# The integer addition that rounds the weights on VectorE, with a mask, four small copies and one weight piece moved, in an mLSTM cell followed by a squared-ReLU network

## The chip, the cores and the metric

The kernel runs on one core of a Trainium2 chip, in one launch. The core has five engines that each work through their own queue in order: PE (TensorE, matrix products), DVE (VectorE), ACT (ScalarE), POOL (GpSimd) and SP (SyncE, which here only issues DMAs). An instruction waits in its queue until the semaphores it names have come, and everything behind it in the same queue waits too. The metric is the device time of the launch in microseconds (us). All arithmetic of the result is in float32; the two weight matrices arrive as float64.

## The reference

What is computed, cut to what matters:

```python
# attention: 4 batches x 8 heads, 768 time steps, head width 40
for t in range(S):
    m_new = np.maximum(f_gate[:, :, t] + m, i_gate[:, :, t])
    f_stab = np.exp(f_gate[:, :, t] + m - m_new)
    i_stab = np.exp(i_gate[:, :, t] - m_new)
    m = m_new
    C = f_stab[:, :, None, None] * C + i_stab[:, :, None, None] * np.einsum('bhd,bhe->bhde', vt, kt)
    n = f_stab[:, :, None] * n + i_stab[:, :, None] * kt
    h_tilde = np.einsum('bhde,bhe->bhd', C, qt)
    denom = np.maximum(np.abs(np.einsum('bhd,bhd->bh', n, qt)[:, :, None]), 1.0)
    y[:, :, t] = 1.0 / (1.0 + np.exp(-o_gate[:, :, t])) * h_tilde / denom
# network: x is y as (3072, 320); w_in (320, 2048), w_out (2048, 320)
h = np.maximum(x @ w_in, 0.0)
return (h * h @ w_out).astype(np.float32)
```

## The kernel before

The recurrence is cut into 24 chunks `s` of 128 time steps (six for each batch). For a chunk the kernel loads keys, queries and values; lays the gates' running sums A along the rows (`load_A`, tile `A_bc`, a DMA); sets the entries above the diagonal to a very small number (`mask`, L414, one or two affine selects on POOL); takes exponentials with the bias `b` (`weigh`, L450, eight ACT instructions at L467, from chunk 8 on at L461 with the turned copy `b_R` of `b_T`); multiplies the scores into them (`weighted`, L542, DVE at L552), which gives P; and multiplies P with the values on PE (`attend`, L554; from chunk 6 on `attend_begin`, L612, and `attend_end`, L671). The state C goes from chunk to chunk on DVE (L586) and POOL (L589, L594), and POOL makes the weighted values `vw` (L481, L487). `normalise` (L733) divides on DVE (L737 to L747) and leaves `x_sb`, which PE turns for the network (`turn_rows`, L772, matmuls at L777).

In `attend_begin` the last DVE instruction, L628, reads one element of a PSUM bank that PE has just written, and the second half of the chunk's matmuls (L666 in `attend_end`) waits for it.

The network runs on groups of two chunks. Groups 0 and 1 go through `ffn1` (PE at L799 and L810, ACT at L823 and L829); later groups through a scheme with fewer products (`ffn1_begin`, `ffn1_open`, `ffn1_rows`, `ffn1_close`; PE at L966 and L1015, ACT at L979 and L1032, DVE at L998 to L1000 and L1033 to L1036).

The weights come as float64. The class `Rounding` turns them into float32 in 18 pieces: pieces 0 to 9 are `w_in` (128 rows x 512 words), pieces 10 to 17 are `w_out` (128 x 640). `fetch` (L201) loads a piece as pairs of 32-bit words, `words` (L211, L213) makes two float arrays `mag` and `low` on ACT, and `join` (L216) clamps `mag` (L222), shifts it (L226), puts the sign in (L227), all on DVE, and adds the words of `mag` and `low` as integers (L231, on POOL); then it fetches the piece four further on. `step` calls `words` so that they stay a piece ahead, then `join`. The array `mag` has two buffers of its own, and every third of the first twelve pieces uses borrowed room instead.

The order is written out by hand: what a Python statement emits first stands first in its engine's queue. A first part handles chunks 0 and 1. The loop over `u` from 0 to 7 (L1137) takes half a chunk at a time, `s = 2 + u // 2`: at even `u` it turns the rows of chunk s-1, takes the scores of chunk s, a quarter of `ffn1`, `weighted(s)` and `weigh(s + 1)`; at odd `u` it runs `attend(s)`, a `join`, `normalise(s)` and another quarter of `ffn1`. The list `NEXT` says how many pieces must be done by the end of each `u`. At u = 0 a `step` stands ahead of `weigh(3)`, and `mask(3)` is called inside `weigh(3)`. Each `fetch` stands in SP's queue behind the loads emitted before it.

After the loop four ACT copies (L1200) write `b_R`. The second loop (L1217) runs over parts `n` of the network, four to a chunk, `s = 6 + n // 4`. At the end of parts 0 to 4 it calls `step` until `LAST[n]` pieces are done, so piece 16 is joined at the end of part 0 and piece 17 at the end of part 2. Part 3 ends with `ffn1_close` of group 2, part 4 begins with `scores(7)` and `weighted(7)`, and part 5 holds `attend_begin(7)`. Parts 4 and 5 multiply with the first and the second half of `w_out` (L836).

Of the kernel before, what the change touches and what calls it, by code (L numbers as in the profile page):

```python
# [10 lines left out]
I32 = mybir.dt.int32  # L11
# [3 lines left out]
ALU = mybir.AluOpType  # L15
# [14 lines left out]
def kernel(  # L30
# [27 lines left out]
    nc = tc.nc  # L58
# [4 lines left out]
    PR = H // 2  # L63
# [110 lines left out]
    class Rounding:  # L174
# [41 lines left out]
        def join(self):  # L216
            n = len(self.b)
            dst = pieces[n][0]
            w = dst.shape[1]
            mag, low = (t[:, :w] for t in self.a[n])  # L220
            bits = mag.bitcast(I32)
            nc.vector.tensor_scalar(  # L222
                mag, mag, scalar1=word_as_float(0x38000000), scalar2=word_as_float(0x47EFFFFF),
                op0=ALU.max, op1=ALU.min,
            )
            nc.vector.tensor_scalar(bits, bits, scalar1=3, scalar2=None, op0=ALU.logical_shift_left)  # L226
            nc.vector.scalar_tensor_tensor(  # L227
                bits, in0=self.raws[n][:, :w, 1], scalar=-0x80000000, in1=bits,
                op0=ALU.bitwise_and, op1=ALU.bitwise_xor,
            )  # L230
            nc.gpsimd.tensor_tensor(dst.bitcast(I32), bits, low.bitcast(I32), op=ALU.add)  # L231
            self.b.append(None)
            if n != LENT - 1:
                self.fetch()
# [186 lines left out]
    def mask(s):  # L421

        A = st[s]["A"][0]
        if s < ROT:
            nc.gpsimd.affine_select(
                A[:], A[:], compare_op=ALU.is_ge, fill=-1e30, base=0, pattern=[[0, H], [1, P]], channel_multiplier=-1,
            )
            return
        for rows in HALVES:
            part = A[rows, :, DP : DP + P].rearrange("p x (late t) -> p x late t", late=2)  # L430
            nc.gpsimd.affine_select(  # L431
                part, part, compare_op=ALU.is_ge, fill=-1e30, base=0, pattern=[[0, PR], [0, 2], [1, DP]],
                channel_multiplier=-1,
            )
# [604 lines left out]
    def ffn1_square():  # L1039
        if "open" in st:  # L1040
# [4 lines left out]
            nc.scalar.activation(g4[:, :, :, P0], g4[:, :, :, P0], AF.Square)  # L1045
            nc.scalar.activation(g4[:, :, :, P1], g4[:, :, :, P1], AF.Square)

    def do(f, s):
        if 0 <= s < NT:
            f(s)  # L1050
# [86 lines left out]
    for u in range(8):  # L1137
        s = 2 + u // 2
        relu_half()
        if u % 2 == 0:  # L1140
            if u == 0:
                ffn1(0, 0)
            else:
                turn_rows(s - 1)
                scores(s)
                ffn1(u // 4, u % 4)
            if u == 2:
                rounding.words()
            weighted(s)
            if u == 0:  # L1150
                rounding.step()
            if u == 2:
                mask(s + 1)
                rounding.join()
                rounding.join()
                weigh(s + 1, masked=True)
                rounding.words()
            else:
                weigh(s + 1)
                square_half()  # L1160
        else:
            load_A(s + 2)
            for r in {1: (4,), 3: (5, 6), 5: (7,), 7: ()}[u]:
                load(r)
            if u == 5:
                for r in range(4, 8):
                    half_tanh(r)
            attend(s)
            if u == 3:
                square_half()  # L1170
            rounding.join()
            normalise(s)
            for r in {5: (8,), 7: (9,)}.get(u, ()):
                load(r)
            for r in {5: (7,), 7: (8,)}.get(u, ()):
                pair_up(r)
            if u > 4:
                load_o(2 * s)
                load_o(2 * s + 1)
            transposes(s + 1)  # L1180
            rounding.words()
            ffn1(u // 4, u % 4)
            square_half()
        if u < 4:
            load_o(4 + u)
        while rounding.done < NEXT[u]:
            rounding.step()
        if u in WIN_SUMS:
            sums_of_win(WIN_SUMS[u])
# [4 lines left out]

    for m in range(2):
        for own in range(2):
            x = PR * (m ^ own ^ 1)
            nc.scalar.copy(b_R[HALVES[m], :, :, own], b_T[HALVES[1 - own], :, :, x : x + PR])  # L1200
    spread_slots(1)
    banks.close()
    ps_h = ctx.enter_context(tc.tile_pool(name="ps_h", bufs=5, space=PSUM))
# [6 lines left out]
    for g in range(1, NG):  # L1210
        parts += [(2, g, i) for i in range(4)]
        if g + 2 < NG:
            parts += [(1, g + 2, i) for i in range(4)]
    LAST = (17, 17, 18, 18, 18)
    assert LAST[-1] == len(pieces)

    for n, (which, g, i) in enumerate(parts):  # L1217
        s, at = 6 + n // 4, n % 4
        if n == 5:
            brought.close()  # L1220
            late = ctx.enter_context(tc.tile_pool(name="late", bufs=1, side="right"))
        even = s >= 8 and s % 2 == 0
        fast = which == 1
        if at == 0:
            if s < 8 or even:
                do(scores, s)
            if even:
                do(turn_kq, s + 1)
            if s < 8 or even:
                do(weighted, s)  # L1230
        if at == 1:
            do(attend_begin, s)
            if even:
                do(lambda s: scores(s, ("h", "h")), s + 1)
            if fast:
                ffn1_rows(g, 0, True)
            do(attend_end, s)
            do(decays, s + 1)
            do(mask, s + 1)
            if n > 4 and not even and not fast:  # L1240
                do(turn_kq, s + 1)
            do(decay_C, s + 1)
            if s > X_SQ and not fast and not even:
                do(turn_squares, s - 1)
            do(store_num, s)
            do(load_num, s)
            do(load_squares, s + 2)
            if even:
                do(load_A, s + 2)
        if 5 <= n < 8:  # L1250
            sums_of_weights(n - 5)
        if n == 6:
            sums(1, slice(0, NPAIR), (1, 2))
        if n == 8:
            sums_of_weights(3)
            sums(1, slice(0, NPAIR), (3,))
        if n == 9:
            sums(1, slice(0, NPAIR), (4,))
        if which == 2 and i == 3 and g == NG - 2:
            sums(g + 1, slice(0, NPAIR), (2,))  # L1260
        if which == 2 and g > 1 and i < 2:
            sums(g, slice(0, NPAIR), (3 + i,))
        if n == 0:
            ffn1_begin(g)
            sums_of_x(g)
            sums_of_win(2)
        if at == 3 and s >= 8 and s % 2 == 0 and s // 2 - 1 < NG:
            sums_of_x(s // 2 - 1)
        if at == 2 and not fast:
            if even:  # L1270
                do(turn_squares, s - 1)
            if n > 4:
                do(scale_q, s + 1)
        if at == 3:
            if s % 4 == 3:
                for r in range(s + 1, min(s + 5, NT)):
                    half_tanh(r)
        if fast:
            if i % 2:
                ffn1_close(g, i // 2, i == 1)  # L1280
                if at == 1 and g > 2:
                    do(turn_kq, s + 1)
                    do(turn_squares, s - 1)
            else:
                ffn1_open(g, i // 2)
                if i == 0 and g > 2:
                    sums(g - 1, slice(0, NPAIR), (2,))
            if at == 2 and g > 2:
                do(scale_q, s + 1)
        elif g == 0:  # L1290
            ffn2(g, *divmod(i, 2))
        else:
            ffn2_fast(g, i)
        if at == 2:
            do(lambda s: weigh(s, masked=True), s + 1)
            ffn1_square()
            if n < 4:
                do(turn_kq, s + 1)
                do(scale_q, s + 1)
            if even:  # L1300
                do(weighted, s + 1)
            do(normalise_turned, s)
            do(store_rows, s)
            if not even:
                do(load_A, s + 2)
            if s > 6:
                do(load_o, s + 5)
            do(load_rows, s)
            if s == 6:
                do(pair_up, s + 3)  # L1310
        if s > 6 and at == (3 if even else 2):
            do(pair_up, s + 3)
        if s > 6 and at == 3:
            if s == 7:
                load(s + 3)
            do(load, s + 4)
        if n in (9, 25):
            spread_slots(2 + n // 25)
        if at == 0:
            ffn1_square()  # L1320
        if n < 5:
            while rounding.done < LAST[n]:
                rounding.step()
# [30 lines left out]
```

## Time and profile before

| what | value |
|---|---|
| median of 3 runs | 500.82 us (500.54 to 502.58) |
| profiled execution, its own time | 498.15 us |
| span of the profiled execution | 496.4 us |
| granted TensorE clock | 1.00 |
| L231 on POOL, 128x512 | x10, about 1.28 us each |
| L231 on POOL, 128x640 | x8, 1.55 us each (median) |
| L227 on DVE, 128x512 and 128x640 | 0.69 and 0.83 us |
| L1200 on ACT | x4, 0.27 us each |
| A_bc load, 512 KB | 5.5 to 6.5 us to landing |

The span is the time between the first and the last instruction on the core; 1.75 us of the execution lie around it. A line of the timeline gives start, duration, engine, source line, operation, output and inputs, shape and count; a bracket at its end says how long the engine was idle before it and what released it. A line of the waits gives the waiting engine and line, the awaited engine and line, the total in us, how often, and the longest.

### The profile page before, as it was taken

What the parts mean: (1) busy time and instruction counts of PE and PEld (TensorE: products, weight loads), DVE (VectorE), ACT (ScalarE), POOL (GpSimd) and SP (SyncE); (2) the same over time, 40 slices, a digit from 0 to 9 for tenths busy, and PEclk for the clock granted to TensorE, in tenths of its full rate; (3) what the DMA queues carried; (4) which work ended last, traced back from release to release, by engine and by line L of the source; (5) the groups of instructions that cost most, each with busy time, mean ns of one, the idle gap of its engine ahead of it and who ended that gap; (6) DMA issues with size and microseconds to landing.
All of it is one profiled execution on the core that took longest, in us unless ns stands there. A gap on an engine that the chain in (4) does not pass through costs nothing.

```text
span 496.4 us, 15227 instructions
## 1 busy us (share of the span) xinstructions
PE 487.0 (98%) x6169; PEld 452.5 (91%) x6169; DVE 346.3 (70%) x700; ACT 241.3 (49%) x530; POOL 224.5 (45%) x317
## 2 busy tenths in 40 slices
PE   9999999999999999999999999999999999999997
PEld 4877878897799999999999999999999999999997
DVE  8598969868977677767866866866866956735441
ACT  3657888754612551581561670561861560423300
POOL 3265744531489458458549438448544030020000
PEclk9999999999999999999999999999999999999999
DMA  9999797756597597688678578677766532200000
GB/s 188 207 229 219 238 217 159 208 90 129 117 188 156 128 174 181 124 152 176 138 144 180 130 145 176 153 138 161 155 125 142 116 74 80 55 15 15 3 26 28
DMA packets 196167, 68.02 MB, mean 137 GB/s; under 512 B 158704, under 2 KB 186064, under 8 KB 196096
## 3 DMA queue, kind: packets, MB, share of 16 engines
q1 hardware_dynamic: 190560, 57.50, 55.9%
q0 software_dynamic: 5440, 9.34, 8.0%
q8 instruction: 49, 0.80, 0.7%
q10 hardware_dynamic: 96, 0.20, 0.2%
q14 instruction: 22, 0.18, 0.1%
HBM read 54.71 MB, written 18.01 MB: 146 GB/s over the span
## 4 chain that ended last, share of the span: by engine, by line
PE 90%; DVE 4%; ACT 2%; issue 1%; DMA 1%; POOL 1%; SPq 0%; DVEq 0%; POOLq 0%; ACTq 0%
PE h_ps L890 35%; PE h_ps L966 24%; PE h_ps L1015 7%; PE h_ps L799 4%; PE h_ps L836 3%; PE numT L655 2%; PE numT L636 2%; PE hp L575 2%; PE idle L1059 1%; PE h_ps L810 1%; PE numT L666 1%; PE tp L530 1%; PE h_ps L530 1%; PE tp L504 1%; PE tp L538 1%
## 5 line engine op out<-in xcount | busy, mean ns | idle before, releaser
L890 PE MATMUL h_ps<-T,S 128*128 128x160 f32 x352 | 51.7, 300 | 0.0
L996 ACT COPY r_sb<-h_ps 128x512 f32<-128x512 f32 x18 | 10.5, 585 | 83.7 <-PE h_ps L966 83.7
L890 PEld LDWEIGHTS h_ps<-T,S 128*128 128x128 f32 x352 | 48.9, 190 | 0.4 <-ACT g_c L1032 0.2
L890 PE MATMUL h_ps<-w_out,g 128*128 128x160 f32 x336 | 49.2, 303 | 0.0
L890 PEld LDWEIGHTS h_ps<-w_out,g 128*128 128x128 f32 x336 | 46.1, 190 | 1.3 <-issue 0.7
L906 DVE TENSOR_TENSOR y_sb<-y_sb,h_ps 128x160 f32<-128x160 f32 x44 | 14.1, 320 | 47.5 <-PE h_ps L890 47.5
L431 POOL TENSOR_SCALAR_AFFINE_SELECT A_bc<-A_bc 64x512 f32<-64x512 f32 x32 | 25.2, 788 | 47.0 <-ACT kq L448 40.7
L966 PE MATMUL h_ps<-xT,w_in 128*128 128x128 f32 x320 | 43.0, 278 | 0.8 <-ACT r_sb L979 0.8
L966 PE MATMUL h_ps<-lent_t,w_in 128*128 128x128 f32 x320 | 42.2, 275 | 0.0
L966 PEld LDWEIGHTS h_ps<-xT,w_in 128*128 128x128 f32 x320 | 38.9, 192 | 2.4 <-issue 1.0
L1015 PE MATMUL h_ps<-xT,w_in 64*64 64x128 f32 x960 | 39.1, 272 | 0.0
L966 PEld LDWEIGHTS h_ps<-lent_t,w_in 128*128 128x128 f32 x320 | 38.9, 192 | 0.2 <-issue 0.2
L966 PE MATMUL h_ps<-lent_t 128*128 128x128 f32 x320 | 39.0, 275 | 0.0
L966 PEld LDWEIGHTS h_ps<-lent_t 128*128 128x128 f32 x320 | 37.3, 192 | 0.0
L461 ACT ACTIVATE A_bc<-A_bc,b_R 128x64 f32<-128x64 f32 (+1 forms) x128 | 35.7, 361 | 1.0 <-POOL A_bc L431 0.5
L1015 PEld LDWEIGHTS h_ps<-xT,w_in 64*64 64x64 f32 x960 | 34.8, 133 | 1.3
L340 POOL DMA_DIRECT2D va<-in_v_dram x56 | 34.3, 619 | 2.5 <-DMA va<-in_v_dram 1.4
L686 DVE STREAM_TRANSPOSE tn<-numT 128x256 f32<-128x256 f32 x36 | 14.0, 428 | 28.6 <-PE numT L636 19.8
L481 POOL TENSOR_TENSOR vw<-va,A_bc 128x328 f32<-128x328 f32 x13 | 10.7, 822 | 50.6 <-ACT A_bc L461 50.5
L799 PE MATMUL h_ps<-xT,w_in 128*128 128x256 f32 x128 | 29.9, 384 | 1.7 <-POOL w_in L231 1.1
L958 POOL TENSOR_TENSOR lent_t<-xT 128x128 f32<-128x128 f32 (+1 forms) x18 | 13.0, 738 | 38.5 <-DVE xT L769 38.5
L799 PEld LDWEIGHTS h_ps<-xT,w_in 128*128 128x128 f32 x128 | 23.5, 190 | 5.8 <-POOL w_in L231 1.5
(200 smaller groups left out, 1191.0 us busy)
## 6 DMA issues: line engine op xcount, KB each, us to landing
A_bc<-a_slots SPq DMA_DIRECT2D x32, 256.0 KB, 4.7
num_rows<-tn SPq DMA_DIRECT2D x18, 256.0 KB, 2.2
kq<-num_rows SPq DMA_DIRECT2D x72, 64.0 KB, 2.0
raw<-in_moe_w_out_dram SPq DMA_DIRECT2D x7, 640.0 KB, 4.2
kqT<-kq_rows SPq DMA_DIRECT2D x34, 128.0 KB, 3.0
og<-in_o_gate_dram SPq DMA_DIRECT2D x24, 160.0 KB, 5.3
out_dram<-y_sb SPq DMA_DIRECT2D x24, 160.0 KB, 3.1
raw<-in_moe_w_in_dram SPq DMA_DIRECT2D x7, 512.0 KB, 5.6
```

Source lines behind the costliest of these rows:

```text
L340: eng.dma_start(dst[HALVES[n], PR * (1 - late_keys) : PR * (2 - late_keys)], src[HALVES[late_keys], PR * m : PR * (m + 1)],)
L431: nc.gpsimd.affine_select(part, part, compare_op=ALU.is_ge, fill=-1e30, base=0, pattern=[[0, PR], [0, 2], [1, DP]], channel_multiplier=-1,)
L461: nc.scalar.activation(A[0][:, x, to], A[0][:, x, to], AF.Exp, bias=b_R[:, b, c, own, x : x + 1],)
L481: nc.gpsimd.tensor_tensor(d["vw"][:].rearrange("p (own x) d -> p own x d", own=2), d["va"][:].rearrange("p (own x) d -> p own x d", own=2) ...
L686: nc.vector.transpose(to[:, 2 * m : 2 * m + 2], d["numT"][m].rearrange("p c t -> p (c t)"))
L799: nc.tensor.matmul(hs[i][:, n, :], lhsT=w_in[:, a, fb * P : (fb + 1) * P], rhs=xT[:, :, a, :], start=(n == 0 and a == 0), stop=False,)
L836: nc.tensor.matmul(o_ps, lhsT=st["g2", g][:, fb, j * P : (j + 1) * P], rhs=w_out[:, fb, :], start=(fb == 0), stop=(fb == NF - 1),)
L890: nc.tensor.matmul(to, lhsT=lhsT[:, p], rhs=rhs[:, p, :], start=(start and p == 0), stop=(p == NPAIR - 1), skip_group_check=True,)
L906: add = lambda to, a, b: nc.vector.tensor_tensor(to, a, b, op=ALU.add)
L958: sub = lambda to, a, b: eng.tensor_tensor(to, a, b, op=ALU.subtract)
L966: nc.tensor.matmul(to[:, n, :], lhsT=lhsT[:, 4 * q + n, :], rhs=rhs, start=(start and n == 0), stop=True, skip_group_check=True,)
L1015: nc.tensor.matmul(to[cols, n, :], lhsT=w_in2[rows, 4 * q + n, cols], rhs=rhs, start=(start and n == 0), stop=True, skip_group_check=True,)
```

## The change

Four edits. The integer addition L231 goes from POOL's queue to DVE's, directly behind L227. At u = 0 `mask(3)` is emitted ahead of the `step` there, no longer inside `weigh(3)`. The four copies into `b_R` become `turn_halves` and are emitted in part 3. Piece 17 is joined at the end of part 4 (behind `weighted(7)`) and no longer at the end of part 2.

```diff
@@ join
-            nc.gpsimd.tensor_tensor(dst.bitcast(I32), bits, low.bitcast(I32), op=ALU.add)
+            nc.vector.tensor_tensor(dst.bitcast(I32), bits, low.bitcast(I32), op=ALU.add)
@@ ahead of do
+    def turn_halves():
+        for m in range(2):
+            for own in range(2):
+                x = PR * (m ^ own ^ 1)
+                nc.scalar.copy(b_R[HALVES[m], :, :, own], b_T[HALVES[1 - own], :, :, x : x + PR])
@@ loop over u
             if u == 0:
+                mask(s + 1)
                 rounding.step()
...
             else:
-                weigh(s + 1)
+                weigh(s + 1, masked=(u == 0))
                 square_half()
@@ between the loops
-    for m in range(2):
-        for own in range(2):
-            x = PR * (m ^ own ^ 1)
-            nc.scalar.copy(b_R[HALVES[m], :, :, own], b_T[HALVES[1 - own], :, :, x : x + PR])
     spread_slots(1)
...
-    LAST = (17, 17, 18, 18, 18)
+    LAST = (17, 17, 17, 17, 18)
@@ loop over n
+        if n == 3:
+            turn_halves()
         if n in (9, 25):
```

On DVE the addition is built as a custom operation over 16-bit elements: 128x1024 where POOL had 128x512 words, 128x1280 where it had 128x640.

## The prediction

> **What bounds the kernel now.** I read the page's busy times first, then PE's waits, then the timeline of 0 to 126 us engine by engine.
>
> ```profile
> PE 487.0 (98%) x6169; PEld 452.5 (91%) x6169; DVE 346.3 (70%) x700; ACT 241.3 (49%) x530; POOL 224.5 (45%) x317
> ```
>
> PE is busy for 487.0 of 496.4 us. About 3.3 us of the rest is the tail after its last matmul, so some 6 us of holes are all that a change off PE can win. PE's waits name the holes:
>
> ```profile
> PE tp L777 <- ACT g L823: 1.2, 1, 1.2
> PE h_ps L799 <- POOL w_in L231: 1.1, 1, 1.1
> PE idle L1059 <- DVE zeros L1054: 0.9, 1, 0.9
> PE h_ps L966 <- ACT r_sb L979: 0.8, 1, 0.8
> PE h_ps L799 <- ACT g L823: 0.6, 1, 0.6
> PE numT L636 <- DVE A_bc L552: 0.5, 1, 0.5
> PE tp L777 <- DVE x_sb L746: 0.4, 1, 0.4
> PE tp L777 <- DVE x_sb L747: 0.4, 1, 0.4
> PE numT L666 <- DVE kq L628: 0.3, 1, 0.3
> ```
>
> By the timeline they lie at 65.39, 50.75, 0.94, 99.71, 44.43, 122.30, 30.56, 31.35 and 123.84 us. From 124 to 400 us PE is never idle, so whatever is won or lost before 124 us stays to the end. The first row is mislabelled: L777 turns `x_sb`, whose L746 ends at 65.24, just ahead of 65.39.
>
> The stretch from 31.2 to 65.5 us holds the most (in order PE, PEld, DVE, ACT, POOL busy):
>
> ```profile
> 31.20:65.50 34.30, 31.30 (x213) 25.75 (x214) 31.27 (x50) 27.47 (x62) 21.60 (x20) 1.00 1.01 231
> ```
>
> DVE is busy for 31.27 of 34.30 us. But it is partly not working:
>
> ```profile
> 62.55 1.54 POOL L231 TENSOR_TENSOR w_out<-mag,low 128x640 int32<-128x640 int32 x1
> 62.66 1.46 DVE L740 SCALAR_TENSOR_TENSOR dm<-num,dm 128x8 f32<-128x8 f32 x1
> ...
> 39.97 1.35 POOL L425 TENSOR_SCALAR_AFFINE_SELECT A_bc<-A_bc 128x1024 f32<-128x1024 f32 x1
> 40.40 1.20 DVE L226 TENSOR_SCALAR lent_t<-lent_t 128x512 int32<-128x512 int32 x1
> ```
>
> L740 takes 0.17 us elsewhere and L226 0.43: each stands still until the POOL instruction ends.
>
> [...]L552 with a PSUM input (0.68 us always) never suffers. [...] No row shows the 16-bit addition.
>
> **The change part by part.**
>
> *The addition's price.* [...] On POOL 10 x 1.28 + 8 x 1.55 = 25 us vanish; on DVE 10 x 0.70 + 8 x 0.83 = 13.6 appear.
>
> *11.7 to 31.2 us.* Pieces 0 and 1 add 1.4 us; DVE idles for 5.6 us between them. Behind piece 1, `normalise(1)` moves 0.2 us, up against the mask of chunk 2, at 28.13 on POOL. If that now blocks L740 in place of L745, `x_sb` of chunk 1 is 0.3 us late for PE; otherwise 0. I take 0.1 lost.
>
> *31.2 to 65.5 us* decides. DVE runs from the first L222 at 31.21 to the end of L747 at 65.47: 34.26 us. Idle in it: 0.46 (for dC) and 1.58 (for ACT), 2.04. Excess over each form's shortest: L222 2.45 (0.59, 1.13, 0.17, 0.56), L226 4.81 (0.95, 0.77, 0.95, 0.76, 0.95, 0.43), L227 0.41, L739 0.17, L740 1.29, L747 0.42, together 9.55. Bare work is 34.26 - 2.04 - 9.55 = 22.67. Pieces 2 to 10 add 8 x 0.70 + 0.83 = 6.43. POOL keeps three `vw` (0.74), two masks (1.09), two pairs Cd and C (1.47), 7.34 us. Now the lock: if none of that blocks DVE, `x_sb` of chunk 3 is ready at 31.21 + 29.10 = 60.3, PE fills its three holes here (0.63 + 1.06 + 1.17) and gains 2.86. If all does, it is ready at 67.6 and PE loses 2.1. Walking the queues by hand with the trace's durations I get hits for nearly all. `vw` of chunk 2 slips in between L227 and the addition of piece 3 (0.65). Chunk 3's A_bc, issued at 31.17, lands 6.5 us later, at 37.7, so its mask meets piece 4 (0.95). Chunk 3's `vw`, Cd and C now meet piece 5 (3 x 0.55) rather than the idle 1.58 us. SP's next loads hang on the L227 of piece 4, which moves from 38.6 to 40.2, so chunk 4's A_bc lands near 47.6 and its mask meets piece 6 (0.95). The last three meet pieces 8 to 10 (1.8). Sum 6.0 (82%; before, 9.55 of 21.6, 44%). L747 then ends at 66.3, L746 at 66.1, and PE resumes 0.7 us later than at 65.39. On the way the hole at 44.43 closes (weigh of chunk 3 ends at 41.5, not 43.8), but `x_sb` of chunk 2 comes at 47.5 for a PE there at 46.8, and piece 6 at 51.0 for a PE that waited until 50.75. I take 0.7 lost, between 2.9 gained and 2.1 lost.
>
> *The mask.* On POOL nothing is left between chunk 2's `vw` and this mask, so once the addition is gone the edit moves no instruction past another: 0.
>
> *65.5 to 97 us.* DVE idles before L552 at 67.03 (1.56) and before L581 at 72.80 (2.69) and 88.20 (1.00). Pieces 11 to 15 (0.83 each, 4.2) fall into these and the L739 and L740 excess of 1.1 to 2.0 us a chunk. Taken at 0; without cover, at most 0.4 at the `x_sb` of chunk 4, which ends at 80.73 for a PE at 80.75.
>
> *The copies.*
>
> ```profile
> 97.93 1.11 ACT L1200 COPY b_R<-b_T 64x96 f32<-64x96 f32 x4
> 99.07 1.07 ACT L979 COPY r_sb<-h_ps 128x512 f32<-128x512 f32 x2
> ```
>
> Without them L979 can start 1.1 us earlier; its input is ready at about 97.9. The hole at 99.71 goes: 0.82 gained. In part 3 they land behind L1032 (115.22), where ACT is idle for 5.86 us ahead of L1043; their reader starts at 129.95. Cost 0.
>
> *Pieces 16 and 17.*
>
> ```profile
> 105.24 0.83 DVE L227 SCALAR_TENSOR_TENSOR mag<-raw,mag 128x640 int32<-128x640 int32 x1
> 106.09 0.16 DVE L628 TENSOR_SCALAR kq<-numT 1x1 f32<-1x1 f32 x1
> ...
> 117.38 0.49 DVE L222 TENSOR_SCALAR mag<-mag 128x640 f32<-128x640 f32 x1
> ...
> 123.63 0.16 DVE L628 TENSOR_SCALAR kq<-numT 1x1 f32<-1x1 f32 x1 [0.78 <-PE numT L666]
> ```
>
> Piece 16's addition stands ahead of L628, which moves from 106.25 (its end) to 107.1; PE wants it at 106.83. Loss 0.3. Piece 17 leaves the stretch ahead of L1033: 119.17 - 117.38 = 1.79 earlier, so P of chunk 7 comes at 121.0 and the hole of 0.52 closes. But behind P the piece takes 1.79 + 0.83 = 2.6, to 123.6, and L628 behind it ends at 123.8, where PE waits again, now with its first half done at 123.04. The hole moves and is not filled: 0 (0.5 gained if the piece is quicker). Part 5 needs the piece at about 126.7, in time.
>
> Sum: 0.1 + 0.7 - 0.82 + 0.3 = 0.3 us slower, 498.15 to 498.4. The runs' median stands 2.7 above the profiled execution; carried to it, 500.82 + 0.3 = 501.1.
>
> **Rivals.** *The lock rarely bites* (faster). If POOL's remaining work blocks DVE at 44% as before, 3.2 us, `x_sb` of chunk 3 ends at 63.5: gain 1.9, in all 2.3; at 20% or less PE's holes all close: -2.86 - 0.82 + 0.3 = -3.4, 497.4. For it: POOL loses over half its work here. Against: DVE loses its idle time, in which those blocks were hidden. [...] *Late DVE starves the fetches*: each `fetch` waits for an L227; it is inside my walk.
>
> **How the numbers follow.** What this kernel's measurement can tell from no change is 0.5%, 2.5 us. Forecast 0.50 (its own range 499.5 to 502.2: DVE's path from 1.6 better to 1.1 worse); the lock seldom bites 0.28 (497.0 to 498.3); slower 0.22 (503.4 to 507.5). For 8 in 10 the range runs from 497.4 to 504.0.
>
> **What would show it.** Right: L231 on DVE at 0.69 and 0.83; the waits L799 on POOL and L966 on L979 gone; a wait of L777 on `x_sb` near 66; L666 on L628 twice. Wrong: the addition above 0.95, or L777 at 63 or earlier, or a new hole after 124 us.

## The result, and the profile after

The changed kernel took 499.52 us (median of 22 runs, 496.96 to 509.31) beside 499.75 us (497.25 to 504.0) for the kernel before, run next to it: a ratio of 0.9984 with a 95% interval of 0.9963 to 1.0006. (Every ratio and every count of runs here leaves out the runs that took over 1.5% longer than the fastest of the same kernel, three of these 22, and so no ratio is the quotient of two medians.) That is no change within the 0.5% that the prediction set as its bound. The profiled span went from 496.4 to 496.8 us.

The page's busy times of the changed kernel show the work that moved. POOL lost 28 us (224.5 to 196.2) and DVE gained 4.1 (346.3 to 350.4), though the eighteen additions alone take 14.9 us there: the rest was time in which DVE instructions had stood still. L226 takes 9.8 us in all for 13.6 before, L739 and L740 together 2.0 for 6.6.

```profile
PE 486.7 (98%) x6169; PEld 452.6 (91%) x6169; DVE 350.4 (71%) x718; ACT 241.7 (49%) x530; POOL 196.2 (39%) x299
```

PE's waits in the changed kernel (waiting line, awaited line, us in total, times, longest):

```profile
PE tp L504 <- DVE num L581: 1.7, 2, 1.5
PE numT L666 <- DVE kq L628: 1.5, 2, 1.3
...
PE tp L777 <- DVE x_sb L747: 0.8, 2, 0.5
PE tp L777 <- DVE x_sb L746: 0.6, 2, 0.3
...
PE h_ps L799 <- DVE w_in L231: 0.3, 1, 0.3
```

Gone are L799 on POOL and on L823, L966 on L979, P of chunk 7, and L777 on the rows of chunk 3. The largest wait in their place is one that the list of before doesn't have, L504 on L581; L628 now holds PE twice, and L777 waits 0.29 and 0.50 us for the rows of chunk 2. Four holes on PE's timeline (start, duration, what, and in the bracket the idle time ahead of it with its releaser):

```profile
50.55 3.29 PE L799 MATMUL h_ps<-xT,w_in 128*128 128x256 f32 x14 [0.30 <-DVE w_in L231]
60.08 1.09 PE L504 MATMUL tp<-ident,kq 128*128 128x128 f32 x8 [1.48 <-DVE num L581]
106.56 0.44 PE L666 MATMUL numT<-vw,kq 64*64 64x41 f32 x16 [0.15 <-DVE kq L628]
123.56 0.44 PE L666 MATMUL numT<-vw,kq 64*64 64x41 f32 x16 [1.33 <-DVE kq L628]
```

As a mark for PE's progress I take the start of its 48 matmuls at L836 behind chunk 7: 124.89 us in the kernel before, 124.61 here. So the whole early stretch, where all four edits act, won 0.28 us.

And DVE's timeline of the changed kernel, where the new hole comes from:

```profile
54.88 0.69 DVE L227 SCALAR_TENSOR_TENSOR lent_t<-raw,lent_t 128x512 int32<-128x512 int32 x1
55.71 1.02 DVE L231 CUSTOM_DVE_ANT_0 w_in<-lent_t 128x1024 uint16<-128x1024 uint16 x1
56.65 0.95 DVE L222 TENSOR_SCALAR mag<-mag 128x512 f32<-128x512 f32 x1
57.63 0.43 DVE L226 TENSOR_SCALAR mag<-mag 128x512 int32<-128x512 int32 x1
58.09 0.69 DVE L227 SCALAR_TENSOR_TENSOR mag<-raw,mag 128x512 int32<-128x512 int32 x1
58.92 0.69 DVE L231 CUSTOM_DVE_ANT_0 w_in<-mag,low 128x1024 uint16<-128x1024 uint16 x1
59.53 0.49 DVE L581 TENSOR_TENSOR num<-hi,eA_T 128x328 f32<-128x328 f32 x1
```

L581 reads `hi`, which PE finished at 55.96 (L561, 54.84 + 1.12). It stands behind pieces 8 and 9 in DVE's queue and starts at 59.53, and only then is the PSUM buffer of `hi` free for PE's next transposes (both take turns in the same three buffers). The addition takes 0.69 us in nine of the ten pieces of 512 words; beside POOL's `vw` (55.22 to 56.17) the one at 55.71 took 1.02.

### The profile page after: what moved, and what is told of

Same layout as the page of the kernel before. It is cut to its first block, busy times and chain, and to the rows that moved or that the text cites. A ratio compares the mean times of both kernels' runs of the same rounds, so it can differ in the third digit from the quotient of the medians.

```text
span 496.8 us, 15232 instructions
## 1 busy us (share of the span) xinstructions
PE 486.7 (98%) x6169; PEld 452.6 (91%) x6169; DVE 350.4 (71%) x718; ACT 241.7 (49%) x530; POOL 196.2 (39%) x299
## 4 chain that ended last, share of the span: by engine, by line
PE 85%; DVE 5%; DMA 4%; SPq 2%; ACT 2%; issue 1%; POOL 0%; DVEq 0%
PE h_ps L890 34%; PE h_ps L966 23%; PE h_ps L1015 6%; PE h_ps L799 4%; PE h_ps L836 3%; PE numT L655 2%; PE numT L636 2%; PE hp L575 1%; PE tp L538 1%; PE numT L666 1%; PE h_ps L810 1%; SPq L706 1%; DMA kqT<-kq_rows 1%; PE tp L530 1%; PE h_ps L530 1%
## 5 line engine op out<-in xcount | busy, mean ns | idle before, releaser
L431 POOL TENSOR_SCALAR_AFFINE_SELECT A_bc<-A_bc 64x512 f32<-64x512 f32 x32 | 23.8, 743 | 57.6 <-ACT kq L448 56.6
L966 PE MATMUL h_ps<-xT,w_in 128*128 128x128 f32 x320 | 42.8, 278 | 0.0
L966 PE MATMUL h_ps<-lent_t,w_in 128*128 128x128 f32 x320 | 42.2, 275 | 0.0
L966 PEld LDWEIGHTS h_ps<-xT,w_in 128*128 128x128 f32 x320 | 38.9, 192 | 1.4 <-issue 1.0
L966 PEld LDWEIGHTS h_ps<-lent_t,w_in 128*128 128x128 f32 x320 | 38.9, 192 | 0.2 <-issue 0.2
L966 PE MATMUL h_ps<-lent_t 128*128 128x128 f32 x320 | 39.0, 275 | 0.0
L966 PEld LDWEIGHTS h_ps<-lent_t 128*128 128x128 f32 x320 | 37.3, 192 | 0.0
L799 PE MATMUL h_ps<-xT,w_in 128*128 128x256 f32 x128 | 29.6, 383 | 0.3 <-DVE w_in L231 0.3
L890 PE MATMUL h_ps<-w_out,g_c 128*128 128x160 f32 x192 | 28.0, 302 | 0.0
```

The source lines that it names most:

```text
L431: nc.gpsimd.affine_select(part, part, compare_op=ALU.is_ge, fill=-1e30, base=0, pattern=[[0, PR], [0, 2], [1, DP]], channel_multiplier=-1,)
L799: nc.tensor.matmul(hs[i][:, n, :], lhsT=w_in[:, a, fb * P : (fb + 1) * P], rhs=xT[:, :, a, :], start=(n == 0 and a == 0), stop=False,)
L890: nc.tensor.matmul(to, lhsT=lhsT[:, p], rhs=rhs[:, p, :], start=(start and p == 0), stop=(p == NPAIR - 1), skip_group_check=True,)
L966: nc.tensor.matmul(to[:, n, :], lhsT=lhsT[:, 4 * q + n, :], rhs=rhs, start=(start and n == 0), stop=True, skip_group_check=True,)
```

## Experiments

Two theories before the first runs. Theory A is the prediction's: the addition costs DVE about what leaving POOL gives back, and the three moves gain on their own. Theory B: taking from POOL 25 us of work that holds DVE up is a gain by itself, and something else eats it. "The lock" is the word of the prediction and the expectations for what the traces show: a DVE instruction stands still beside a POOL instruction, as L227 at 43.13 in the changed kernel, which took 1.25 us beside POOL's L594 (42.89 to 43.83) and 0.69 at its shortest. C stands in each expectation for the rival of that run.

### The addition alone, and the moves alone

`e1_add_only` is the kernel before with the first diff line of the change and nothing else; `e2_moves_only` is the changed kernel with that line undone:

```diff
-            nc.vector.tensor_tensor(dst.bitcast(I32), bits, low.bitcast(I32), op=ALU.add)
+            nc.gpsimd.tensor_tensor(dst.bitcast(I32), bits, low.bitcast(I32), op=ALU.add)
```

> Kernel before with the addition on VectorE and nothing else changed (mask inside weigh, copies between the loops, piece 17 at the end of part 2). Theory A (VectorE's own path paces PE up to 66 us; the lock relief only just pays for the additions there): L777 of chunk 3 comes 0.4 us later than before, the hole of 0.8 at L966 behind L979 stays, L628 behind piece 16 costs 0.3, and piece 17 with its addition ahead of P of chunk 7 widens the hole there from 0.5 to 1.3; in all 1.5 us slower than before (ratio 1.003). Theory B [...]: 1 to 2 us faster than before (ratio 0.996 to 0.998).

> The changed kernel with the addition put back on GpSimd; mask, copies and piece 17 stay moved. Theory A: chunk 3's mask now runs ahead of piece 4's addition, so the 0.6 hole at 44 us closes, ScalarE comes earlier to piece 6 and the 1.1 hole at 50.75 shrinks to 0 to 0.5; L979 0.8 gained; piece 17 without an addition on VectorE ends at 122.8 and L628 is in time, 0.5 gained; in all 2 to 3 us faster than before (ratio 0.994 to 0.996), and so 1.5 to 2.5 us faster than the changed kernel. Theory B: within 0.8 us of before (ratio 0.998 to 1.001).

The addition alone: 503.02 us, ratio 1.0069 (1.0037 to 1.0100). The moves alone: 498.14 us, ratio 0.9963 (0.9940 to 0.9985). So B falls: the addition on DVE is a loss by itself, and larger than A had it. PE's timeline of the addition alone, and its stretches (busy times of PE, PEld, DVE, ACT, POOL, then the granted TensorE clock, DMA share and GB/s), say why it is larger:

```profile
59.34 1.94 PE L504 MATMUL tp<-ident,kq 128*128 128x128 f32 x8 [1.48 <-DVE num L581]
61.07 4.49 PE L799 MATMUL h_ps<-xT,w_in 128*128 128x256 f32 x16
```

```profile
55.00:61.00 6.00, 4.52 (x34) 4.41 (x34) 5.76 (x9) 3.46 (x6) 2.57 (x3) 0.87 0.64 204
61.00:67.00 6.00, 6.00 (x29) 4.53 (x27) 3.82 (x10) 3.30 (x6) 0.65 (x1) 0.85 0.94 214
```

The hole of 1.48 us is the changed kernel's. But behind it the clock fell, and the same eight transposes take 1.94 us where the changed kernel's took 1.09; the next sixteen matmuls take 4.49 where 3.62 is usual. That is 1.7 us on top of the hole. Single executions stand up to 1.4 us apart before any edit acts, so I count from the scores of chunk 2 to the mark: the addition alone needs 95.66 us (31.20 to 126.86) where the kernel before needs 93.28 (31.61 to 124.89), 2.38 more, and without the 1.7 it would be 0.7 (an estimate). The moves alone need 90.92 (30.24 to 121.16), 2.36 less.

### No addition, and the addition twice

`e3_no_add` is the changed kernel without the addition, so L227 writes the weights itself (and L226 shifts by 0); `e4_add_twice` issues it a second time:

```diff
@@ e3_no_add
-                bits, in0=self.raws[n][:, :w, 1], scalar=-0x80000000, in1=bits,
+                dst.bitcast(I32), in0=self.raws[n][:, :w, 1], scalar=-0x80000000, in1=bits,
...
-            nc.vector.tensor_tensor(dst.bitcast(I32), bits, low.bitcast(I32), op=ALU.add)
@@ e4_add_twice
-            nc.vector.tensor_tensor(dst.bitcast(I32), bits, low.bitcast(I32), op=ALU.add)
+            for _ in range(2): nc.vector.tensor_tensor(dst.bitcast(I32), bits, low.bitcast(I32), op=ALU.add)
```

> The changed kernel without the integer addition on any engine: the sign instruction L227 writes the weights straight into their place and the shift L226 shifts by 0, so the low words are left out and the weights have other values; every other instruction is as in the changed kernel. Theory A: VectorE's path is 6.4 us of additions shorter by 66 us, PE's holes at 44, 50, 60 and 65 us all close, and L628 waits only about 0.5 us behind piece 17 and not at all behind piece 16: 3.5 to 4.5 us faster than before (ratio 0.991 to 0.993). Theory C (the holes do not hang on VectorE's path, but on loads and on ScalarE): less than 1.5 us faster than before.

> The changed kernel with each integer addition done twice on VectorE, one right behind the other, the same result written again. Theory A: another 6.4 us on VectorE's path by 66 us, nearly all of it on PE's as well, 0 to 1 us between 66 and 97, and 0.8 more at each of the two L628: 7 to 9 us slower than the changed kernel (ratio to before 1.013 to 1.018). Theory C: hidden but for the two L628, 1.5 to 3 us slower than the changed kernel.

Without it: 495.4 us, ratio 0.9913 (0.9882 to 0.9944), mark 119.82. Twice: 512.53 us, ratio 1.0260 (1.0223 to 1.0297), mark 136.64. So the first set of additions costs 0.7% and the second 2.8%, four times as much. PE's timeline and stretches of the doubled one:

```profile
64.49 1.97 PE L504 MATMUL tp<-ident,kq 128*128 128x128 f32 x8 [3.31 <-DVE num L581]
...
117.02 0.61 PE L666 MATMUL numT<-vw,kq 64*64 64x41 f32 x16 [1.95 <-DVE kq L628]
135.59 0.44 PE L666 MATMUL numT<-vw,kq 64*64 64x41 f32 x16 [1.32 <-DVE kq L628]
```

```profile
61.00:67.00 6.00, 2.69 (x12) 2.48 (x12) 5.69 (x10) 1.09 (x3) 0.99 (x1) 0.63 0.79 249
67.00:75.00 8.00, 8.00 (x47) 6.14 (x47) 6.03 (x12) 4.89 (x11) 2.03 (x2) 0.85 1.44 175
```

Over half of the second set's price is the clock, 0.63 and 0.85 in these stretches. One minus a run's mean granted clock, times its span, estimates what it lost to the clock; I call it the shortfall. On average it is 0.7 us without the addition, 1.5 in the changed kernel and 8.8 with the addition doubled. So some 7.3 of the second set's 13.8 us (2.8%) are the clock's, and 0.8 of the first set's 3.6. What is left, 6.5 and 2.8, is still twice as much for the second set, which found less idle and standing time on DVE; neither is paid in full, since ten additions at 0.69 and eight at 0.83 are 13.5 us. A is right in direction and rank in both; its 7 to 9 us for the second set left the clock out, and without the clock 6.5 is near them. (Without the addition the weights have other values; whether that bears on the clock is not shown.)

### Each move by itself, on the kernel before

`e6_mask_only`, `e7_copies_only` and `e8_piece17_only` each take one of the other three edits of the change, with the addition on POOL:

```diff
@@ e6_mask_only
+                mask(s + 1)
                 rounding.step()
...
-                weigh(s + 1)
+                weigh(s + 1, masked=(u == 0))
@@ e7_copies_only: the loop of four copies behind the loop over u
-                nc.scalar.copy(b_R[HALVES[m], :, :, own], b_T[HALVES[1 - own], :, :, x : x + PR])
...
+        if n == 3:
+            turn_halves()
@@ e8_piece17_only
-    LAST = (17, 17, 18, 18, 18)
+    LAST = (17, 17, 17, 17, 18)
```

> The kernel before with chunk 3's mask ahead of the step at u = 0, and nothing else. Theory A (with the addition on POOL, the mask waited there behind piece 4, and the exponentials of chunk 3 behind it): the wait of L777 at 44.43 us (0.63) goes, and PE stands 0.3 to 0.8 us earlier at 66 us; ratio to before 0.998 to 1.000. Theory C (the place of the mask costs nothing, as the prediction put it for the changed kernel): PE stands within 0.2 us of before at 66 us.

> The kernel before with the four copies of b in part 3, and nothing else. Theory A (they delay L979 by 1.1 us, and their new place is idle): the wait of L966 on L979 (0.82 at 99.71 us) goes, no wait appears in part 3 or behind, and PE stands 0.8 us earlier at 120 us; ratio to before 0.998 to 0.999. Theory C (another input of L966 is late anyway): a wait of 0.3 us or more stays at L966.

> The kernel before with piece 17 joined at the end of part 4, and nothing else; its addition stays on POOL. Theory A (the DVE part of the piece, 1.8 us, fits between P of chunk 7 and L628): the wait of 0.52 us for P of chunk 7 goes and that at L628 (0.28 at 123.84) goes too, PE stands 0.5 to 0.8 us earlier at 125 us; ratio to before 0.998 to 0.999. Theory C (the hole moves to L628 as it did with the addition on DVE): a wait of 0.3 us or more at L628 and PE within 0.3 us of before.

*The mask*: 498.38 us, ratio 0.9962 (0.9941 to 0.9984), more than A gave it, and about all that the three moves gain together. The timelines of POOL and ACT with the mask alone:

```profile
36.32 1.28 POOL L425 TENSOR_SCALAR_AFFINE_SELECT A_bc<-A_bc 128x1024 f32<-128x1024 f32 x1
...
37.64 2.46 ACT L467 ACTIVATE g_c<-A_bc,b_T 128x128 f32<-128x128 f32 x8 [0.77 <-POOL A_bc L425]
```

Before, the mask ran at 39.97 and the exponentials at 41.35, behind piece 4's addition on POOL. With the exponentials 3.7 us earlier the hole of 0.63 at 44.43 is gone, and the one at L799 fell from 1.06 to 0.70. From the scores of chunk 2 to L777 of chunk 3 PE needs 32.54 us (30.83 to 63.37) for 33.78 (31.61 to 65.39).

*The copies*: ratio 0.9987 (0.9960 to 1.0014), too small for the runs. In the trace the wait at L966 is gone and none appears in part 3: PE goes from L777 of chunk 5 to L836 in 20.55 us (96.57 to 117.12) for 21.59 (95.26 to 116.85). The mark itself, 125.19, is not early as A had it: behind the hole of 1.16 at L777 of chunk 3 the clock was 0.80 from 67 to 75 us in this execution.

*Piece 17*: ratio 1.0004 (0.9976 to 1.0031). The wait for P of chunk 7 is gone; a wait of 0.58 at L628 stays, which A said would go. From L836 to the mark PE needs 7.23 us (118.11 to 125.34) for 8.04, so A's sum holds and not its claim that all holes close. The mark itself, 125.34, is late for the same reason as with the copies (the stretch stands at the end of this document).

By the runs the three moves sum to -0.38 - 0.13 + 0.04 = -0.47%, and together they measured -0.37%.

### Pieces 16 and 17 added on POOL

`e5_tail_on_pool` is the changed kernel with one line edited:

```diff
-            nc.vector.tensor_tensor(dst.bitcast(I32), bits, low.bitcast(I32), op=ALU.add)
+            (nc.gpsimd if n > 15 else nc.vector).tensor_tensor(dst.bitcast(I32), bits, low.bitcast(I32), op=ALU.add)
```

> The changed kernel with the additions of pieces 16 and 17 back on POOL, the other sixteen on DVE. Theory A (behind these two pieces the addition itself delays L628): both waits of PE at L666 on L628, 0.33 us at 106.56 and the one at 123.56, go, and PE stands 0.4 to 1.0 us earlier at 124 us than with the changed kernel: ratio to before 0.996 to 0.998. Theory C (the tail has cover, and the loss is all before 66 us): both waits shrink by under 0.2 us together and PE stands as with the changed kernel.

Ratio 0.9989 (0.9960 to 1.0018): the runs don't tell it from the changed kernel. In the trace the first wait at L628 is gone and the second fell from 1.33 to 0.36; from the second half of chunk 6 (first L666) to the mark PE needs 19.01 us (107.22 to 126.23) for 20.36 (104.25 to 124.61). So behind these two pieces the addition costs 1.35 us, more than A's 0.4 to 1.0. The mark itself is late, 126.23, because in this execution the clock fell behind the 1.58 us hole at L504 (0.57 from 61 to 67 us).

### The new hole

`e10_piece9_later` is the changed kernel with piece 9 behind L581 and L586, and so piece 10 behind `normalise` of chunk 3:

```diff
-    NEXT = (5, 8, 10, 11, 12, 13, 14, 16)
+    NEXT = (5, 8, 9, 11, 12, 13, 14, 16)
...
             if u == 2:
                 mask(s + 1)
                 rounding.join()
-                rounding.join()
```

> The changed kernel with piece 9 joined at u = 3 (behind attend of chunk 3), and so piece 10 behind normalise of chunk 3. Theory A (the 1.48 us hole at L504 comes from L581 queued behind two joins): that hole goes, L799 waits 0.4 to 1.3 us for piece 9 in its place, L777 of chunk 3 comes 0.2 to 1.1 us earlier than with the changed kernel; ratio to before 0.996 to 0.999. Theory C (L581 is late for another reason, its input or the lock): a hole of 1 us or more stays at L504.

PE's timeline:

```profile
60.29 3.29 PE L799 MATMUL h_ps<-xT,w_in 128*128 128x256 f32 x14 [0.72 <-DVE w_in L231]
64.58 0.55 PE L777 MATMUL tp<-ident,x_sb 128*128 128x128 f32 x3
...
98.30 5.47 PE L966 MATMUL h_ps<-xT,w_in 128*128 128x128 f32 x32 [2.14 <-ACT g L823]
```

The hole at L504 is gone, 0.72 at L799 came for it, and L777 is 1.24 us earlier (64.58 for 65.82): that L581 was late because of the pieces ahead of it is shown. Yet the ratio is 1.0012 (0.9979 to 1.0044; A had 0.996 to 0.999, and the interval still reaches into it). In the trace a new hole of 2.14 us opens at 98.30, with a clock of 0.72 from 98 to 104 us. ACT's timeline names it:

```profile
95.81 0.79 ACT L211 ACTIVATE mag<-raw 128x640 f32<-128x640 f32 x1 [2.13 <-DVE w_out L231]
...
97.18 1.07 ACT L823 ACTIVATE g<-h_ps 128x512 f32<-128x512 f32 x2
```

With the pieces one place later, ACT stands in L211 for a free `mag` buffer, which an addition on DVE must release, and L823 behind it frees PE's PSUM late.

### Two better orders

`e11_moves_swap` is the moves alone with the second of these edits; `e9_mixed` has both:

```diff
@@ e9_mixed
-            nc.gpsimd.tensor_tensor(dst.bitcast(I32), bits, low.bitcast(I32), op=ALU.add)
+            (nc.vector if n in (5, 6) else nc.gpsimd).tensor_tensor(dst.bitcast(I32), bits, low.bitcast(I32), op=ALU.add)
@@ both
-            rounding.join()
-            normalise(s)
+            if u == 3: normalise(s)
+            rounding.join(); (u == 3) or normalise(s)
```

> The three moves with every addition on POOL, and at u = 3 normalise ahead of the join. Theory A: the hole of 1.17 us at L777 of chunk 3 goes, those of 0.76 and 0.89 stay, PE stands 0.9 to 1.2 us earlier at 124 us than with the moves alone; ratio to before 0.993 to 0.995. Theory C (the lock moves the loss): a hole of 0.6 us or more between 55 and 70 us.

> The three moves, with the addition on POOL except for pieces 5 and 6, which are added on DVE, and at u = 3 normalise ahead of the join. Theory A (each of the three holes left with the moves alone is one late item: x_sb of chunk 2 behind piece 5's addition on POOL 0.76, piece 6 itself 0.89, x_sb of chunk 3 behind piece 10 1.17): they shrink to under 0.8 us together, no hole over 0.6 is left, PE stands 2 to 3 us earlier at 124 us than with the moves alone (121.2), ratio to before 0.990 to 0.993. Theory C (the lock moves the loss elsewhere): holes of 1.5 us or more in sum stay and the ratio is not under 0.995.

`e11_moves_swap`: 495.21 us, ratio 0.9899 (0.9841 to 0.9957), mark 120.45. `e9_mixed`: 496.77 us, ratio 0.9916 (0.9874 to 0.9957), mark 119.72. Both beat the kernel before and lie under the changed kernel's interval; their own intervals overlap. PE's timeline of the second:

```profile
48.35 3.29 PE L799 MATMUL h_ps<-xT,w_in 128*128 128x256 f32 x14 [0.17 <-DVE w_in L231]
61.96 0.55 PE L777 MATMUL tp<-ident,x_sb 128*128 128x128 f32 x3
```

L777 of chunk 3 waits no more in either; the holes of 0.76 at chunk 2's rows and 0.89 at L799 shrank to none and 0.17 in `e9_mixed`, and were none and 0.69 in `e11_moves_swap`, with piece 5 and 6 still on POOL. A's reading of the 1.17 is shown (the swap alone closes it); of the 0.76 it isn't, since that hole went without the edit made for it, and ahead of the swap. The moves alone, then the swap:

```profile
46.04 0.52 PE L777 MATMUL tp<-ident,x_sb 128*128 128x128 f32 x3 [0.76 <-DVE x_sb L746]
46.37 0.55 PE L777 MATMUL tp<-ident,x_sb 128*128 128x128 f32 x3
```

So the swap is judged from these rows on. From there to the mark PE needs 75.12 us with the moves alone (46.04 to 121.16), 74.08 with the swap (46.37 to 120.45) and 73.81 with both edits (45.91 to 119.72): the swap gives 1.04, and DVE for two pieces 0.27. A had the mark 0.9 to 1.2 us earlier with the swap and 2 to 3 with both; it came 0.71 and 1.44 earlier. By the runs, six and thirteen, the two kernels lie 0.6% and 0.5% under the moves alone; the traces account for a third and about half of that. A's forecast that no hole over 0.6 is left missed: L628 waits 0.61, and ahead of the edits L777 of chunk 1 waits 0.90 (1.05 with the swap alone).

### Filling the holes

That the clock falls behind a hole was seen, not tested. `e12_holes_filled` tests it on the changed kernel:

```diff
-            transposes(s + 1)
-            rounding.words()
+            if u == 3: idle(3)
+            transposes(s + 1); rounding.words()
...
-            do(attend_end, s)
+            idle(2) if n == 5 else None; do(attend_end, s)
```

> The changed kernel with idle matmuls on PE (0.44 us each) in its two longest holes: three ahead of the transposes L504 of chunk 4 (hole of 1.48 us) and two ahead of the second half of chunk 7 (1.33). They are shorter than the holes, so PE goes on at the same events. Theory A (a hole above about a microsecond often brings the granted clock down for some microseconds after it): of the changed kernel's runs 3 in 19 had a mean granted clock of 0.999 or more; here at least half have, and the median falls 0.7 to 1.5 us under the changed kernel's, ratio to before 0.995 to 0.997. Theory C (the clock falls for another reason): the share stays under 30% and the ratio between 0.998 and 1.001.

The idle matmuls ran faster than in the expectation, and covered about 0.6 and 0.4 us; 0.88 and 0.94 of the two holes stayed. The mean granted clock was 0.999 or more in 11 of 22 runs, where it was in 3 of 19 of the changed kernel's, as A had it. The median didn't follow: 499.07 us, ratio 0.9984 (0.9956 to 1.0013), as for the changed kernel itself, and A's 0.7 to 1.5 us are not shown. The falls summed in the last section cost 1.7 or 3.4 us in a profile, so at 1.7 with the runs under 0.999 going from 16 of 19 to 11 of 22 about 0.6 us was to be expected (an estimate), which this interval can't tell from nothing. So the link from hole to clock is supported; what it costs the median of the changed kernel is open.

## Why the prediction was right

Forecast was no change, 501.1 us from 500.82; measured was no change, -0.16% (-0.37% to +0.06%). The 1.6 us between 501.1 and 499.52 are mostly the kernel before, which stood at 499.75 in this series. By the steps:

- **The addition's price** came as forecast: 0.69 and 0.83 us in the median (three of the eighteen, each beside a POOL instruction, took 1.02 to 1.57). The forecast was the author's estimate, for no row of before shows the operation. An addition above 0.95, which the prediction held possible, falls with it. Not priced was the start: L231 begins 0.83 us after L227 (58.09 to 58.92), where the next instruction behind an L227 began 0.61 after it, so a 512 piece costs DVE 0.83 and not 0.70, and a 640 piece 0.96 for 0.83 (0.96 and 0.75 from start to start, 61.95 to 62.91 to 63.66, for the 0.75 of one instruction alone): 9 x 0.13 = 1.2 us more up to 65.5.
- **31.2 to 65.5 us**: the sum came out near, from two errors that cancel. The additions took 7.6 and not 6.43; the blocks took 4.2 (excess over each form's shortest: L227 0.43 and 0.56, L222 0.50, 0.14 and 0.53, L226 0.41 and 0.56, L747 0.77, L231 0.33) and not 6.0, and 0.56 more was idle for ACT ahead of piece 2's addition. By these three terms the end of L747 would stay at the 66.3 that was forecast; it came at 65.91, and the other 0.4 us are not accounted for. `x_sb` of chunk 3 came at 65.67 (65.18 + 0.49) for 66.1, and L777 at 65.82: 0.43 lost for 0.7. The term is right, its place is not: the prediction followed DVE's queue to `normalise` and never asked who waits for L581 on the way. PE was late by 1.48 us at L504, and so found `x_sb` ready. It was this step, "resumes 0.7 us later than at 65.39" for want of `x_sb`, that named the wrong wait.
- **The holes on the way** went as walked: 44.43 closed, `x_sb` of chunk 2 at 47.15 (forecast 47.5; its last part, L747, only at 48.15), piece 6 at 50.50 with PE at 50.55 (51.0), chunk 3's mask at 37.54 (37.7).
- **11.7 to 31.2 us**: 0.1 lost was forecast; L777 of chunk 1 came at 30.59 for 30.56. Nothing was lost that a single execution can show.
- **The mask at 0** holds for the changed kernel: with the addition alone it ran at 36.79 without being moved. It was worth 0.38% only while the addition stood on POOL. Two edits of this change buy the same microsecond; that is read from these traces, for the changed kernel without this edit was not run.
- **The copies** gained as forecast: L966 runs in one piece from 97.27, and the copies lie at 115.62 beside idle ACT.
- **Pieces 16 and 17**: L628 ended at 106.51 (107.1 was forecast), with PE 0.27 early where it had been 0.60 early at L966: 0.33 lost, for 0.3. Piece 17 moved the hole from P of chunk 7 to L628 and filled nothing, to 123.51 for 123.8: 0, as forecast. The first half was done at 122.2, not 123.04, so the hole reads 1.33.
- **After 124 us** nothing was expected. The profiled execution lost 0.6 us behind 360 us, where a late load (`kqT<-kq_rows`, 5.0 us to landing, 3.0 the median) holds PE; in four profiles of other kernels PE waits longer than that at other places (1.4 to 1.8 us, last section), so it isn't the change's.

The sum at the mark was +0.3 and is -0.28. Both are too small for the runs: the verdict was right, and the closeness owes as much to misses that cancel as to the walk. The rival of the rare lock would have shown L777 at 63 or earlier. It fell, though DVE stood still for less than forecast: 4.2 us, 58% of POOL's 7.34 for 82%. What that left, the additions took.

The lock is read from the traces alone: each of the nine blocks above stands beside POOL's `vw`, mask, Cd or C (L747 took 0.97 us for 0.20 at its shortest beside the mask at 46.90, L222 0.95 for 0.42 beside Cd at 56.14), and the 16-bit addition is held up too, 1.02 us beside `vw`. What makes DVE wait is not shown.

What stays open is why the parts don't add up in the medians: +0.69% and -0.37% would be +0.32%, and the whole measured -0.16%. In the traces the moves' gain mostly overlaps with the addition's (the mask, and piece 17's hole that comes back at L628), which makes the sum worse and not better; the addition alone has the clock's fall in each of its runs (below). Its shortfall is 2.5 us on average, that of the moves alone 1.2 and of the changed kernel 1.5; with the kernel before at about 1 in each series (an estimate: in the changed kernel's own its clocks were not kept) this would be 0.2 of the 0.48%. The three intervals together allow about 0.4%, so there may be nothing left to explain.

## What to carry to other kernels

When work moves into a queue, list every instruction that now stands behind it and who waits for each, not only the last one of the stage; here the result that was followed came in time, and a small instruction that frees a PSUM buffer came late. Try each edit of a bundle alone and against the others: the edit meant to lead was the loss here, and one that was worth 0.38% alone found nothing left to gain beside it. With an engine that is 98% busy, put what frees its buffers ahead of bulk work that is not yet needed, as `normalise` ahead of piece 10: in the traces one swapped pair of lines gave 1.0 us, the whole change 0.3.

## What was not expected of the hardware

A hole on PE can cost more than itself: behind the 1.48 us at L504 of the addition alone the fall of the clock took another 1.7. Over 64 runs of the kernel before, taken in one series, the mean granted clock was 0.999 or more in 37, with a median of 499.45 us, and lower in the other 27, with 501.75. Their shortfall, 2.0 us on average for 0.1, is most of that. By kernel, the share of runs at 0.999 or more:

| kernel | runs at 0.999 or more | longest hole from 2 to 126 us in its profile (each) |
|---|---|---|
| before | 37 of 64 | 1.17 |
| moves alone, mask, copies, piece 17 | 47 of 85 | 1.17; 1.17; 1.16; 1.18 |
| `e9_mixed`, `e11_moves_swap` | 13 of 19 | 0.90; 1.05 |
| no addition | 8 of 10 | 0.53 |
| changed | 3 of 19 | 1.48 |
| `e5_tail_on_pool`, `e10_piece9_later` | 5 of 27 | 1.58; 2.14 |
| addition alone, addition twice | 0 of 16 | 1.48; 3.31 |
| holes filled | 11 of 22 | 0.94 |

In the other three series where its clocks were kept, the kernel before has 17 of 34, 12 of 23 and 15 of 26, so the series don't make the difference. All kernels with a small share have most additions on DVE, so these rows alone can't tell the hole from the addition; the last row has the additions there too, and speaks for the hole.

Where the clock falls is seen in the profiles that have it, within some microseconds behind a hole: 0.72 from 98 to 104 us in `e10_piece9_later`, whose hole ends at 98.30. Summed over the stretches behind such holes, the shortfall is 1.7 us with the addition alone, the moves alone, the copies, piece 17 and `e10_piece9_later`, and 3.4 in `e5_tail_on_pool` and `e9_mixed`. With the addition twice it is 3.4 from 61 to 75 us; the mean clock of 0.985 over 511.0 us makes 7.7 for the whole profile. The other six have a mean clock of 0.999 or more. Behind 126 us, which the table leaves out, PE waits for L552 for 1.4 to 1.8 us in four profiles (the moves alone, `e9_mixed`, the addition alone and twice); behind that hole the clock was 0.81 from 180 to 187 us in the moves alone and 0.73 from 180 to 190 in `e9_mixed`. One hole doesn't decide it: the kernel before went on at 1.00 behind its 1.17 at 65.39, and the kernel with piece 17 alone, behind 1.18 at the same place, fell. Their stretches, the kernel before first:

```profile
67.00:75.00 8.00, 8.00 (x54) 6.93 (x55) 4.71 (x9) 7.51 (x19) 2.83 (x3) 1.00 1.24 229
```

```profile
67.00:75.00 8.00, 8.00 (x43) 6.46 (x41) 3.11 (x6) 5.88 (x15) 2.24 (x2) 0.80 1.21 233
```

PE is busy for all 8 us in both, but gets through 54 recorded matmuls in one and 43 in the other. What decides whether a hole brings the clock down is not shown. It fell behind holes of 1.16 to 3.31 us, and stayed at 1.00 behind others of that size: 1.17 in the kernel before and 1.48 in the changed one, from 61 to 75 us in both.
